# Signs of converted weights: a rectifier of slope -2^32 on ScalarE in place of a VectorE step

## The chip, the cores and the metric

The kernel runs on one core of a Trainium2 chip. The time is the device time of one execution in microseconds (us). The engines are TensorE (PE in the profile, with PEld for its weight loads), VectorE (DVE), ScalarE (ACT), GpSimd (POOL) and SyncE (SP, which issues the DMAs).

## The reference

Attention with 4 batches, 8 heads, 576 positions and 64 dimensions per head, then two layers with hidden width 2048 on the 2304 tokens of width 512. The first layer's activation is Mish, the second's h * clip(h + 3, 0, 6) / 6.

```python
scores = scale * q @ k.T                     # scale = 1 / 8
thresh = max(scores, -1) - tau               # tau = 0.02
scores = where(scores >= thresh, scores, -1e9)
attn = exp(scores - max) / (sum + 1e-9)
x = (attn @ v) -> [2304, 512]
h = x @ w_in;  g = h * tanh(softplus(h));            x = g @ w_out      # first layer
h = x @ w_in2; g = h * clip(h + 3, 0, 6) / 6;        out = g @ w_out2   # second layer
```

## The kernel before

The matrix products run on float16 parts: each operand is split into a high part and the rest, and the products of the parts are added in PSUM. In the second layer sums and differences of quarters are multiplied in place of the quarters, so that its weights need combined parts (`combined`).

The weights lie in memory as float64 words of 64 bits. Each of the four matrices (m = 0 and 1 for the first layer, 2 and 3 for the second) is converted on the chip in 8 groups, so there are 32 conversions, all by `one_conversion`. For one group the 64-bit words are loaded (`raw`, tile raw_lr), DVE finds the largest magnitude (L785), and a scale for the group follows: a diagonal of the per-partition values (L756 on ACT or L758 on DVE, tile dgb_zd), a product with ones on PE that spreads it over partitions (L761), a maximum on DVE (L764) and a few short steps (L796 to L810). Then, into a tile of 128 x 1024 words (cvt_c):

- `c1`, ACT, L921: the high 32-bit halves, read as float32, times the group's scale.
- `c2`, POOL (L929) or DVE (L931), one half of the tile each: shift left by 3, which moves the exponent of float64 to the place of that of float32, and clears the sign bit.
- `c3`, DVE, L937: the sign bit of the raw words is put in.
- `c4`, DVE, L942: the top bits of the low 32-bit halves are put in.
- For m below 2, ACT makes the float16 high part (L961) and POOL or DVE the rest. For m = 2 and 3, sums of quarters (`q`), high parts on ACT (L997) and rests follow.

The work around it changes in time. From about 30 to 140 us the softmax of attention and the conversions of m = 0 run together: PE makes scores (L1849, s_s), DVE the maximum (L1858) and the thresholded step (L1871, e_ex), ACT the exponential (L1868). Up to about 414 us the conversions of m = 1 follow, beside attention and the first product of the first layer, whose results ACT or DVE scales (L1290 and L1292, he_t) and SP stores. From then to about 640 us `first_layer` runs its second half: per unit of 512 columns ACT computes Mish (L1327, hp_e), ACT the float16 high part (L1330, gs_h), DVE the rest (L1336, gs_h), and PE 24 matmuls (L1356, y_y); a block of tokens has 8 units, and there are 72. The results are split again for the second layer (L1111, L1117, L1128). The conversions of m = 2 and 3 lie in this stage, 16 in all. Then the second layer runs (L1430, L1458, L1517, L1523, L1533).

Each engine's instructions stand in an order that a planner (`Plan`) sets when the kernel is built: every step is a `task` with a cost per engine, dependencies, buffers and a due time, shifted by a table of numbers (`NUDGE`). The planner gives each step to the engine that it thinks free first. Engines execute their rows in that order and wait by semaphores. Tiles come from rings of a few buffers: hp_e has 2 in the late stage, gs_h 2 of 4 units each.

ACT computes by tables that it holds in sets. The kernel asks for one set at its start (L699), in which the exponential lies. The program loads another by an instruction of its own, ACT_TABLE_LOAD, where the next activation isn't in the set that ACT holds.

Of the kernel before, what the change touches and what calls it, by code (L numbers as in the profile page):

```python
# [8 lines left out]
F32 = mybir.dt.float32  # L9
# [6 lines left out]
AF = mybir.ActivationFunctionType  # L16
ALU = mybir.AluOpType
# [81 lines left out]
JOIN_FROM = 340.468  # L99
STAY = 0.954  # L100
NBLK_EARLY = 2 * B - 2
NUDGE = {
# [407 lines left out]
class Plan:  # L510
# [19 lines left out]
    def add(  # L530
        self, engines, fn, deps=(), bufs=(), prio=None, off=0.0, dma=0.0, name="", order=()
    ):
        shift = NUDGE.get(name, 0.0)
        prio, off = (None, off + shift) if prio is None else (prio + shift, off)
# [149 lines left out]
def fused_kernel(ctx: ExitStack, tc, q, k, v, tau, w1i, w1o, w2i, w2o, out):  # L684
    nc = tc.nc
# [42 lines left out]
    def sub(e, dst, a, b):  # L728
        engine[e].tensor_tensor(dst, a, b, ALU.subtract)  # L729

    def pick(which, **cost):
        return {e: cost[e] for e in WHO[which]}
# [14 lines left out]
    def bits(t):  # L747
        return t.bitcast(U32)
# [24 lines left out]
    wt, r_w, converted, scaled_by, wsc = {}, {}, {}, {}, {}  # L773

    def high(raw):
        return bits(raw.tile).rearrange("p a (n t) -> p a n t", t=2)[:, :, :, 1]
# [96 lines left out]
    def tasker(at):  # L873
        def task(engines, fn, deps, bufs, tag, dma=0.0):
            return add(engines, fn, deps, bufs, at, 0.0 if at is not None else MOE_OFF, dma, tag)

        return task
# [7 lines left out]
    def convert(m, src, pool, prio, off, ring):  # L885
        if m not in wsc:
            scale_columns(m)
        if m < 2:
            r_w[m] = Ring(f"w{m}_", maker(pool, f"w{m}_", [P, 2, 2, DM], F16), NG)
            wt[m] = [Buf(r_w[m]) for _ in range(NG)]  # L890
            for w in wt[m]:
                w.left += 1
        elif m == 2:
            r_w[m] = Ring(f"w{m}_", maker(pool, f"w{m}_", [P, 7, 2 * P], F16), 2 * NG)
        if m > 1:
            wt[m] = [(Buf(r_w[m]), Buf(r_w[m])) for _ in range(NG)]

        factors = []
        for g in range(NG):
            at = prio + 2 * g * off  # L900
            task = tasker(at)
            raw = Buf(r_raw)
            a = loaded = load_words(task, raw, src[g], f"lr{m}_{g}")
            a = maximum(task, f"{m}_{g}", raw, wsc[m]["top"][:, g : g + 1], a)
            factors.append(group_scale(task, f"{m}_{g}", m, g, ring, a))
            one_conversion(m, g, raw, [loaded, factors[g]], task)
        if m == 0:
            step = NG // len(scaled_parts)
            scaled_parts[:] = [factors[i : i + step] for i in range(0, NG, step)]
        scaled_by[m] = summary(tasker(prio + 2 * NG * off), m, ring, factors)  # L910

    def one_conversion(m, g, raw, deps, task):
        nm = f"{m}_{g}_"
        t = Buf(r_cvt)
        dst = wt[m][g]

        def low():
            return bits(raw.tile).rearrange("p a (n t) -> p a n t", t=2)[:, :, :, 0]

        def c1(e):  # L920
            nc.scalar.activation(  # L921
                t.tile.bitcast(F32), high(raw).bitcast(F32), AF.Copy,
                scale=wsc[m]["sc"][:, g : g + 1],
            )

        def c2(e, j):
            if e == "pool":
                ti = t.tile[:, j].bitcast(I32)
                nc.gpsimd.tensor_tensor(ti, ti, eight.to_broadcast([P, DM]), ALU.mult)  # L929
                return  # L930
            nc.vector.tensor_scalar(  # L931
                t.tile[:, j], t.tile[:, j], 3, 0x7FFFFFF8, ALU.logical_shift_left,
                ALU.bitwise_and,
            )

        def c3(e):
            nc.vector.scalar_tensor_tensor(  # L937
                t.tile, high(raw), 0x80000000, t.tile, ALU.bitwise_and, ALU.bitwise_or
            )

        def c4(e):
            nc.vector.scalar_tensor_tensor(  # L942
                t.tile, low(), 29, t.tile, ALU.logical_shift_right, ALU.bitwise_or
            )

        a = task(EXPAND, c1, deps, [raw, t], "c" + nm)
        b = [
            task(
                pick(f"c{m}{j}", **SHIFT) if m > 1 else SHIFT, lambda e, j=j: c2(e, j), [a], [t],
                f"c{nm}{j}",  # L950
            )
            for j in range(2)
        ]
        a = task({"dve": 1.28}, c3, b, [raw, t], "c" + nm)
        a = task({"dve": 1.28}, c4, [a], [raw, t], "c" + nm)
        if m > 1:
            combined(m, g, t, a, task)
            return

        def hi(e):  # L960
            nc.scalar.activation(dst.tile[:, :, 0], t.tile.bitcast(F32), AF.Copy)  # L961

        def lo(e, j):
            sub(e, dst.tile[:, j, 1], t.tile[:, j].bitcast(F32), dst.tile[:, j, 0])

        a = task({"act": 1.05}, hi, [a], [t, dst], "h" + nm)
        for j in range(2):
            converted[m, 2 * g + j] = task(
                {"pool": 1.25, "dve": 0.68}, lambda e, j=j: lo(e, j), [a], [t, dst], f"u{nm}{j}"
            )  # L970
# [289 lines left out]
    def inner(blk, early, at=None, gap=0.0):  # L1260

        task = planner(at, gap, f"0_{blk}")
        if blk == 2 * B:
            x, src = Buf(r_x), Buf(r_sum)

            def tails_of():
                return src.tile

            def get(e):
                nc.sync.dma_start(out=tails_of(), in_=td)  # L1270

            a = task({"sp": 0.5}, get, tails, [src], "xt", 1.46)
            ready = [
                split(task, f"0_{blk}", src, tails_of, x, xinv[:, B:], r_h, [a])
            ]
            input_scales(B, ready[0], None if at is None else at)
        else:
            x, ready = x_of.pop(blk)
        hscale, scaled = hin[:, blk // 2], hin_done[blk // 2]
        for fp in range(NG):  # L1280
            h = Buf(r_h)
            last = gemm1(task, 0, fp, PIECE if early else 12, x, h, ready)
            if fp % 2 == 0:
                he = Buf(r_he)
                taken = []

            def take(e, h=h, he=he, fp=fp):
                dst, f = he.tile[:, fp % 2], hscale[:, fp : fp + 1]
                if e == "act":
                    nc.scalar.activation(dst, h.tile, AF.Copy, scale=f)  # L1290
                else:
                    nc.vector.tensor_scalar(dst, h.tile, f, None, ALU.mult)  # L1292

            taken.append(task(TAKE, take, [last, scaled[fp]], [h, he], f"t{fp}", 0.0, fp + VECTOR))
            if fp % 2:

                def put(e, he=he, fp=fp):
                    nc.sync.dma_start(out=hd[blk][:, fp // 2], in_=he.tile)

                h_stored[blk, fp // 2] = task(  # L1300
                    {"sp": 0.5}, put, taken, [he], f"s{fp}", HD_DMA, fp + VECTOR
                )
# [761 lines left out]
    t = 0  # L2064
# [3 lines left out]
    for b in range(B):  # L2068
        units = [(hp, cs) for cs in halves for hp in range(NPAIR)]
        tiles = {}  # L2070
        for i, (hp, cs) in enumerate(units):
# [4 lines left out]
            t = tiles[hp](t, cs)  # L2076
# [3 lines left out]
            blk = 2 * b + (i == len(units) - 1)  # L2080
            if (i == len(units) - 1 or i == NPAIR - 1) and blk < NBLK_EARLY:
                pending.append((blk, START + (t + MOE_LAG) * STEP, span * STEP * RATE / NG))
    for blk in range(NBLK_EARLY, NBLK):
        inner(blk, False)
# [60 lines left out]
    task = tasker(at)  # L2145
# [81 lines left out]
```

## Time and profile before

| | |
|---|---|
| median of 3 runs | 985.71 us (985.18 to 986.22) |
| the profiled execution | 984.73 us, span 982.9 us |
| PE busy | 922.2 us (94%) |
| DVE busy | 797.9 us (81%) |
| ACT busy | 650.8 us (66%) |
| POOL busy | 409.2 us (42%) |
| mean granted clock of TensorE | 0.974 |

The span is that of the instructions on the core; the execution's own time is 1.8 us longer. Busy time is a sum over an engine's instructions. An engine that is busy for all of a stretch sets its length; one that is idle there has a reason, which the waits name.

### The profile page before, as it was taken

Reading aid. Unit: us, or ns where it says so; the run is one execution under the profiler, and the core shown is the slowest. Engines: PE = TensorE matmul, PEld = TensorE weight load, DVE = VectorE, ACT = ScalarE, POOL = GpSimd, SP = SyncE. Lnnn points to the kernel's source line nnn. Section 1 sums busy time; section 2 is a strip of 40 time slices with the busy share of each in tenths; the row PEclk is TensorE's granted clock in tenths of the full one; section 3 lists DMA queues with packets and bytes.
Section 4 is the critical chain, followed back from the end, with each engine's and each line's share of the span. In section 5 each row is a group of like instructions: output and inputs, shape, how many; then the busy total and the mean of one; then the engine's idle time right before and its main releaser. Section 6 shows DMA issues by size and latency. Waiting matters only on the chain.

```text
span 982.9 us, 25896 instructions
## 1 busy us (share of the span) xinstructions
PE 922.2 (94%) x10776; PEld 797.2 (81%) x10776; DVE 797.9 (81%) x1516; ACT 650.8 (66%) x1051; POOL 409.2 (42%) x354
## 2 busy tenths in 40 slices
PE   3669779999999999999999999999999999999996
PEld 1447457777777778888888888899999999999986
DVE  6998898888878888569999889888758758758864
ACT  6678688888888877567866778655444444545541
POOL 2777776766655667315656777720000000000000
PEclk9769789999999999999999999999999999999999
DMA  9899999999999999864654757750110110110001
GB/s 313 179 233 234 228 226 218 251 253 217 238 217 270 216 220 238 234 239 173 239 211 176 282 188 287 246 219 9 60 47 16 60 41 22 60 32 31 23 15 31
DMA packets 201798, 164.48 MB, mean 167 GB/s; under 512 B 174160, under 2 KB 174928, under 8 KB 195280
## 3 DMA queue, kind: packets, MB, share of 16 engines
q1 hardware_dynamic: 201680, 162.82, 61.1%
q8 instruction: 85, 1.39, 0.6%
q14 instruction: 33, 0.27, 0.1%
HBM read 84.28 MB, written 36.04 MB: 122 GB/s over the span
## 4 chain that ended last, share of the span: by engine, by line
PE 76%; DVE 13%; POOL 3%; DMA 3%; issue 2%; ACT 1%; SPq 0%; DVEq 0%; POOLq 0%; ACTq 0%
PE h_g L1241 15%; PE y_y L1356 13%; PE s_s L1849 7%; PE aux_pv L1897 5%; PE hp_g1a L1430 5%; PE h_g0a L1430 5%; PE hp_g1d L1430 2%; PE h_g0d L1430 2%; DMA pt_tr<-p_ph 2%; DVE e_ex L1871 2%; DVE nm_pk L1858 1%; POOL p_ph L729 1%; DVE top L785 1%; PE h_g1b L1430 1%; DVE gs_h L1336 1%
## 5 line engine op out<-in xcount | busy, mean ns | idle before, releaser
L729 POOL TENSOR_TENSOR p_ph<-e_ex,p_ph 128x128 f16<-128x128 f32 (+3 forms) x160 | 192.5, 1225 | 106.4 <-issue 54.8
L1583 PEld LDWEIGHTS <-gs_h 128*128 128x128 f16 x1512 | 146.8, 98 | 18.0 <-issue 1.5
L1430 PEld LDWEIGHTS <-w__h 128*128 128x128 f16 x2016 | 156.0, 98 | 1.2 <-issue 0.6
L1871 DVE SCALAR_TENSOR_TENSOR e_ex<-s_s,thr_th,e_ex 128x576 f32<-128x576 f32 x144 | 111.9, 812 | 15.3 <-ACT thr_th L1863 11.8
L1858 DVE TENSOR_REDUCE nm_pk<-s_s 128x1 f32<-128x576 f32 x144 | 104.6, 751 | 18.0 <-PE s_s L1849 17.0
L1868 ACT ACTIVATE e_ex<-s_s,nm_pk 128x576 f32<-128x576 f32 x144 | 104.1, 730 | 18.5 <-DVE nm_pk L1858 13.9
L1849 PE MATMUL s_s<-kd_lk,qs_qp 64*128 64x288 f32 x440 | 80.8, 480 | 36.4 <-DVE e_ex L1871 25.6
L1876 ACT ACTIVATE p_ph<-e_ex 128x576 f16<-128x576 f32 x144 | 94.8, 678 | 13.5 <-DVE e_ex L1871 9.1
L1430 PEld LDWEIGHTS <-w__u 128*128 128x128 f16 x1008 | 98.6, 98 | 0.0
L1897 PEld LDWEIGHTS <-pt_tr 128*128 128x128 f16 x2016 | 81.3, 103 | 11.1 <-issue 5.8
L1849 PEld LDWEIGHTS s_s<-kd_lk,qs_qp 64*128 64x128 f32 x440 | 41.4, 204 | 59.0 <-issue 39.5
L1897 PE MATMUL aux_pv<-vh,pt_tr 128*128 128x65 f16 (+1 forms) x1296 | 86.1, 203 | 1.9 <-DMA pt_tr<-p_ph 1.9
L729 DVE TENSOR_TENSOR gs_h<-g_ab,gs_h 128x896 f16<-128x896 f32 x72 | 74.6, 1087 | 15.9 <-ACT gs_h L1533 15.9
L1533 ACT ACTIVATE gs_h<-g_ab 128x1792 f16<-128x1792 f32 x36 | 59.6, 1690 | 27.4 <-DVE g_ab L729 27.4
L1897 PE MATMUL aux_pv<-vl_vl,pt_tr 128*128 128x64 f16 x720 | 70.7, 203 | 0.0
L1517 ACT ACTIVATE g_ab<-g_ab,aux,hscales 128x512 f32<-128x512 f32 x72 | 54.1, 804 | 16.9 <-DVE g_ab L1458 16.9
L1327 ACT ACTIVATE hp_e<-hl_l 128x512 f32<-128x512 f32 x72 | 42.4, 594 | 23.5 <-DVE gs_h L1336 23.2
L1290 ACT ACTIVATE he_t<-h_g,hin 128x512 f32<-128x512 f32 x63 | 42.9, 683 | 19.0 <-PE h_g L1241 15.1
L1523 DVE SCALAR_TENSOR_TENSOR g_ab<-g_ab,f 128x512 f32<-128x512 f32 x72 | 51.2, 747 | 5.0 <-ACT g_ab L1517 5.0
L1336 DVE SCALAR_TENSOR_TENSOR gs_h<-hp_e,fscales,gs_h 128x512 f16<-128x512 f32 x72 | 53.0, 743 | 2.1 <-ACT gs_h L1330 2.1
L1330 ACT ACTIVATE gs_h<-hp_e,fscales 128x512 f16<-128x512 f32 x72 | 47.3, 678 | 7.6 <-PE y_y L1356 6.8
L1448 ACT ACTIVATE s_ka<-h_g0a 128x512 f32<-128x512 f32 x27 | 16.1, 595 | 48.1 <-PE h_g0a L1430 47.9
(672 smaller groups left out, 2559.2 us busy)
## 6 DMA issues: line engine op xcount, KB each, us to landing
hd<-he_t SPq DMA_DIRECT2D x36, 512.0 KB, 4.2
hl_l<-hd SPq DMA_DIRECT2D x18, 1024.0 KB, 5.7
raw_lr<-in_moe_w_in SPq DMA_DIRECT2D x16, 1024.0 KB, 6.0
raw_lr<-in_moe_w_out SPq DMA_DIRECT2D x16, 1024.0 KB, 7.5
yd<-yl_zhy SPq DMA_DIRECT2D x9, 896.0 KB, 3.8
qs_qp<-in_q SPq DMA_DIRECT2D x10, 576.0 KB, 5.8
v_lv<-in_v SPq DMA_DIRECT2D x16, 320.0 KB, 4.7
kd_lk<-in_k SPq DMA_DIRECT2D x15, 288.0 KB, 3.9
```

What stands on the lines that cost most here:

```text
L729: engine[e].tensor_tensor(dst, a, b, ALU.subtract)
L1241: mm(hv[:, j, :], wj[:, wl, c * P : (c + 1) * P], x.tile[:, c, xl, :], start=j == 0 and n == 0, stop=j == 1 and n == 11, skip_group_check= ...
L1336: nc.vector.scalar_tensor_tensor(s.tile[:, k, 1], g.tile.rearrange("p (a n) -> p a n", a=2), fs[:, fp : fp + 1], s.tile[:, k, 0], ALU.mult ...
L1356: mm(yv[:, h, :], wt[1][f // 2].tile[:, f % 2, wl, c * P : (c + 1) * P], gs[fp // COL].tile[:, fp % COL, gl, f % 2, :], start=fp == 0 and ...
L1430: mm(dst.tile[:, i * Q : (i + 1) * Q], wt[2][fp][wl].tile[:, right - 1, c * P : (c + 1) * P], x[xl].tile[:, c, left - 1], start=first and ...
L1583: mm(region(p), part[:, gl, left - 1], wt[3][fp][wl].tile[:, right - 1], start=fp == n == 0 and spot(p)[1] == 0, stop=fp == NG - 1 and n == 2,
L1849: mm(s[j].tile[:, half, :HALF], lh[r], rh[r], start=m == 0, stop=m == len(terms) - 1,)
L1858: nc.vector.tensor_reduce(neg.tile[:, j : j + 1], sv(j), AX.XY, ALU.max, negate=True)
L1868: nc.scalar.activation(ev(j), sv(j), AF.Exp, bias=neg.tile[:, j : j + 1])
L1871: nc.vector.scalar_tensor_tensor(ev(j), sv(j), thr.tile[:, j : j + 1], ev(j), ALU.is_ge, ALU.mult)
L1876: nc.scalar.activation(p16.tile[:, js, :S], e_.tile[:, js], AF.Copy)
L1897: mm(ov[:, dst, :d], pt.tile[:, j, ch, :], part.tile[:, src, vc, :], start=i == j == ch == 0 and part is vh, stop=j == w - 1 and ch == 8, ...
```

## The change

`c1` becomes a parametric rectifier (Prelu): with the group's scale applied, positive values stay, and negative ones are multiplied by -2^32. So the result is never negative, and a value that was negative has an exponent larger by 32. The shift by 3 of `c2` moves that bit of the exponent to bit 31, the sign, and the mask on DVE now keeps it. `c3` is left out: its task stays in the plan with the same cost, and issues nothing.

```diff
+NEGATIVE = -(2.0 ** 32)
...
+    def idle(e):
+        pass
+
...
         def c1(e):
             nc.scalar.activation(
-                t.tile.bitcast(F32), high(raw).bitcast(F32), AF.Copy,
-                scale=wsc[m]["sc"][:, g : g + 1],
+                t.tile.bitcast(F32), high(raw).bitcast(F32), AF.Prelu,
+                scale=wsc[m]["sc"][:, g : g + 1], alpha=NEGATIVE,
             )
...
             nc.vector.tensor_scalar(
-                t.tile[:, j], t.tile[:, j], 3, 0x7FFFFFF8, ALU.logical_shift_left,
+                t.tile[:, j], t.tile[:, j], 3, 0xFFFFFFF8, ALU.logical_shift_left,
                 ALU.bitwise_and,
             )
-
-        def c3(e):
-            nc.vector.scalar_tensor_tensor(
-                t.tile, high(raw), 0x80000000, t.tile, ALU.bitwise_and, ALU.bitwise_or
-            )
...
-        a = task({"dve": 1.28}, c3, b, [raw, t], "c" + nm)
+        a = task({"dve": 1.28}, idle, b, [raw, t], "c" + nm)
```

The orders of PE, POOL and SP are the same. Lines of the changed kernel are shifted by one or so.

DVE, at the first conversion of m = 0 (cvt_c_0, in attention), before:

```order
L764 TENSOR_REDUCE top_146<-aux_zp_1_1_414 128x1
L1967 TENSOR_SCALAR den_dt_0_2_430<-aux_pv_0_0_1_306 128x4
L937 SCALAR_TENSOR_TENSOR cvt_c_0__1_377<-raw_lr_0_0_199,cvt_c_0__1_377 128x1024
L1970 RECIPROCAL den_dt_0_2_430<-den_dt_0_2_430 128x4
L799 TENSOR_SCALAR top_146<-top_146 128x1
L800 TENSOR_SCALAR sc_147<-top_146 128x1
```

The same place of DVE after the change:

```order
L765 TENSOR_REDUCE top_146<-aux_zp_1_1_414 128x1
L1966 TENSOR_SCALAR den_dt_0_2_430<-aux_pv_0_0_1_306 128x4
L1969 RECIPROCAL den_dt_0_2_430<-den_dt_0_2_430 128x4
L800 TENSOR_SCALAR top_146<-top_146 128x1
L801 TENSOR_SCALAR sc_147<-top_146 128x1
```

The row of `c3` is gone and its neighbours have closed up. So it is at all 32 conversions: DVE has 1422 rows in place of 1454.

ACT, at the last conversion of m = 2 (cvt_c_7, beside the Mish units hp_e of the first layer), before:

```order
L1330 ACTIVATE gs_h_0_4_1_8104<-hp_e_0_4_1_8090,fscales 128x512
L997 ACTIVATE w__h_6_0_2_8112<-cvt_c_6__1_7988 128x768
L921 ACTIVATE cvt_c_7__1_8130<-raw_lr_7_0_7903,sc_6626 128x1024
L1327 ACTIVATE hp_e_0_4_1_8164<-hl_l_0_4_0_7832 128x512
L997 ACTIVATE w__h_6_0_2_8112<-sum_q_6_0_1_8109 128x1024
L1117 ACTIVATE yl_zhy_2_0_2_1_8182<-xf_zvy_2_0_2_1_8059 128x1792
```

The same place of ACT after the change:

```order
L1329 ACTIVATE gs_h_0_4_1_8081<-hp_e_0_4_1_8067,fscales 128x512
L996 ACTIVATE w__h_6_0_2_8089<-cvt_c_6__1_7966 128x768
L925 ACT_TABLE_LOAD
L925 ACTIVATE cvt_c_7__1_8107<-raw_lr_7_0_7881,sc_6610 128x1024
L1326 ACT_TABLE_LOAD
L1326 ACTIVATE hp_e_0_4_1_8141<-hl_l_0_4_0_7811 128x512
L996 ACTIVATE w__h_6_0_2_8089<-sum_q_6_0_1_8086 128x1024
L1116 ACTIVATE yl_zhy_2_0_2_1_8159<-xf_zvy_2_0_2_1_8036 128x1792
```

The activations stand in the same order. A table load stands before the rectifier and one before the next Mish, and so at each of the 16 conversions of m = 2 and 3, some with a few activations between the rectifier and the second load. At the 16 conversions of m = 0 and 1 ACT has no new row. ACT has 977 rows in place of 945.

## Rows read from the trace of the kernel before

**Rows 1.** The page: busy us of each engine, its share, its instructions.

```profile
PE 922.2 (94%) x10776; PEld 797.2 (81%) x10776; DVE 797.9 (81%) x1516; ACT 650.8 (66%) x1051; POOL 409.2 (42%) x354
```

**Rows 2.** Busy time by stretch: length, PE, PEld, DVE, ACT, POOL, PEclk, DMA share, GB/s.

```profile
30.00:140.00 110.00, 79.94 (x821) 57.86 (x817) 99.41 (x210) 81.86 (x144) 80.85 (x74) 0.78 0.94 221
140.00:432.00 292.00, 289.73 (x3466) 231.91 (x3466) 240.18 (x447) 232.08 (x431) 174.66 (x157) 1.00 1.02 235
432.00:610.00 178.00, 175.81 (x1617) 157.23 (x1616) 164.92 (x278) 135.46 (x201) 118.21 (x84) 1.00 0.60 215
```

**Rows 3.** Waits from 30 to 140 us: total us, times, longest.

```profile
PEld s_s L1849 <- issue: 23.9, 17, 4.5
PE s_s L1849 <- DVE e_ex L1871: 19.9, 10, 4.1
PEld s_s L1849 <- DVE e_ex L1871: 5.4, 3, 4.7
```

**Rows 4.** Waits from 432 to 610 us.

```profile
ACT hp_e L1327 <- DVE gs_h L1336: 21.3, 23, 3.7
...
PE h_g L1241 <- DVE he_t L1292: 2.1, 1, 2.1
```

**Rows 5.** Busy time of L937 (`c3`) alone, by stretch: length, DVE, PEclk, DMA share, GB/s.

```profile
30.00:140.00 110.00, 10.82 (x8) 0.78 0.94 221
140.00:432.00 292.00, 9.72 (x8) 1.00 1.02 235
432.00:640.00 208.00, 24.09 (x16) 1.00 0.61 222
sum 610.00, DVE 44.63; mean DVE 14.88
```

**Rows 6.** Timeline of DVE at two early sign steps: start us, us; idle before.

```profile
34.23 1.23 DVE L937 SCALAR_TENSOR_TENSOR cvt_c__1_377<-raw_lr,cvt_c__1_377 128x1024 uint32<-128x1024 uint32 x1 [0.37 <-POOL cvt_c__1_377 L929]
35.37 0.17 DVE L1970 RECIPROCAL den_dt<-den_dt 128x4 f32<-128x4 f32 x1
...
111.29 1.43 DVE L937 SCALAR_TENSOR_TENSOR cvt_c__1_1405<-raw_lr,cvt_c__1_1405 128x1024 uint32<-128x1024 uint32 x1 [1.67 <-POOL cvt_c__1_1405 L929]
```

**Rows 7.** Chain of waits from 440 to 535 us: start us, us, what.

```profile
470.18 3.07 DVE cvt_c__1_7392 L937
...
494.37 3.14 DVE cvt_c__1_7780 L937
...
530.01 1.47 PE h_g L1241 x12
```

**Rows 8.** The page's costliest groups: busy us, mean ns; idle before, releaser.

```profile
L1517 ACT ACTIVATE g_ab<-g_ab,aux,hscales 128x512 f32<-128x512 f32 x72 | 54.1, 804 | 16.9 <-DVE g_ab L1458 16.9
L1327 ACT ACTIVATE hp_e<-hl_l 128x512 f32<-128x512 f32 x72 | 42.4, 594 | 23.5 <-DVE gs_h L1336 23.2
L1290 ACT ACTIVATE he_t<-h_g,hin 128x512 f32<-128x512 f32 x63 | 42.9, 683 | 19.0 <-PE h_g L1241 15.1
```

**Rows 9.** Timeline of ACT at its one table load after the start.

```profile
413.10 0.69 ACT L1290 ACTIVATE he_t<-h_g,hin 128x512 f32<-128x512 f32 x1 [1.98 <-PE h_g L1241]
413.81 1.28 ACT L1327 ACT_TABLE_LOAD   x1
415.10 1.12 ACT L1327 ACTIVATE hp_e<-hl_l 128x512 f32<-128x512 f32 x2
416.16 1.25 ACT L1330 ACTIVATE gs_h<-hp_e,fscales 128x512 f16<-128x512 f32 x2
```

**Rows 10.** Timeline of DVE and of PE: one Mish unit finished, then used.

```profile
605.07 0.73 DVE L1336 SCALAR_TENSOR_TENSOR gs_h<-hp_e,fscales,gs_h 128x512 f16<-128x512 f32 x1
...
610.14 2.78 PE L1356 MATMUL y_y<-gs_h,w__h__1_5966 128*128 128x256 f16 x24
```

**Rows 11.** Timeline of ACT and of PE: one diagonal written, then used.

```profile
475.61 0.39 ACT L756 ACTIVATE dgb_zd<-ident,top 128x128 bf16<-128x128 f32 x1
...
476.07 0.22 PE L761 MATMUL h_zp<-dgb_zd,ones 128*128 128x128 bf16 x1
```

## The prediction, made blind

> **What bounds the kernel now.** I read first the busy time of each engine [rows 1]: TensorE (PE) is busy for 922.2 of 982.9 us, 94%, so an operation taken off another engine is worth something only where PE waits. I therefore cut the span at the places where the converted weights are used, and read busy time by stretch [rows 2]. From 140 to 432 us PE is busy for 289.73 of 292.00 us, from 432 to 610 us for 175.81 of 178.00 us. Only from 30 to 140 us is it open: 79.94 of 110.00 us, with a mean granted clock of 0.78. So 2.3 and 2.2 us are all that a shorter VectorE (DVE) could win in the last two stretches, and the first is where it could win more. There PE waits 19.9 + 5.4 us for DVE's softmax step, and 23.9 us for nothing that the profile shows [rows 3].
>
> For the loss I read the other side of the same rows: from 432 to 610 us ScalarE (ACT) is busy for 135.46 of 178.00 us, so it is idle for 42.5 us. Its largest wait, 21.3 us in 23 pieces, is for DVE to have used the Mish tile [rows 4]. The ring of these tiles is short, so ACT can't run ahead there.
>
> **What is removed.** The 32 sign steps on DVE (L937) cost 10.82, 9.72 and 24.09 us in the three stretches, 44.63 us in all [rows 5]. An undisturbed one takes 1.23 us and the next instruction starts 1.13 us after it: 34.23 to 35.37 us [rows 6].
>
> *Early, eight steps.* 8 x 1.13 = 9 us of DVE time. The waits for POOL in front of two of them, 0.37 and 1.67 us [rows 6], also move to L942, which stands later. PE waits there for DVE (25.3 us) about as long as for nothing shown (23.9 us) [rows 3], so I count half: -4 us. The bounds are 0 (something else is late next: ACT's exponential, or the transfers, whose share in that stretch is 0.94 [rows 2]) and -10 us (all of it, and one wait).
>
> *Middle, eight steps.* PE has 2.3 us open in 292, so 0, with bounds -2 and 0. What covers the old step is PE's own work.
>
> *Late, sixteen steps.* 24.09 us of DVE. The two slowest stand with 3.07 and 3.14 us in the chain of waits that leads to PE's h_g at 530.01 us [rows 7], where PE has its one longer stop, 2.1 us behind DVE's L1292 [rows 4]. That stop can go: -2 us at most, the open time of PE.
>
> **What is added.** The activation itself has the same shape and also a scale from a tile. I price it like the Copy that it replaces. From the nearest rows: at 128x512 a Copy with a scale from a tile takes 683 ns, a Mish without one 594 ns, and a rectifier that takes scale and bias from tiles 804 ns [rows 8]. Carried to 128x1024 by doubling the differences that is between -0.18 and +0.24 us each, for 16 late ones -2.8 to +3.9 us of ACT time; I take 0, since the Copy row is the nearest in its operands.
>
> The order shows what else comes: 32 loads of an activation table, two around each of the late 16 conversions, one before the rectifier and one before the next Mish, and none in the first 16, where ACT still holds the set of the start. Before, there was one load at this place: he_t starts at 413.10 us and lasts 0.69, the load starts at 413.81 and lasts 1.28, the Mish starts at 415.10 [rows 9]. So it costs 1.28 us, 0.03 us of gaps, and the 0.06 us or so by which ACT's neighbours otherwise overlap (1.12 us of Mish from 415.10, next at 416.16): 1.37 us. 32 x 1.37 = 44 us on ACT, 41 of it from 432 to 610 us (15 of the 16 conversions), against 42.5 us of idle time. ACT would be about full there.
>
> The Trainium skill, "ScalarE: Activation LUTs", section "What ACT_TABLE_LOAD costs", gives 1283 ns for the load, as the trace has it, and adds a drain of about 1380 ns to each switch of sets. This trace shows no such drain at its one switch. By the page the 32 loads would take an estimated 85 us of ACT; the rival of the doubled load below is the mechanism, worked out from rows.
>
> *What the 41 us do to PE.* Queued behind a late conversion on ACT are the Mish (L1327) and its rounding (L1330) for the units to come, the diagonals for the group scales (L756, which PE's L761 waits for) and he_t (L1290, PE's h_g). Two kinds of slack stand against it. A finished Mish unit waits for PE: the unit that DVE finishes at 605.07 + 0.73 = 605.80 us is first used at 610.14, 4.3 us later [rows 10]. Over the 72 units that slack is 2.6 to 15.5 us, typically 8, and 5 near the end. The diagonal has none: at 475.61 us ACT writes it, at 476.07 PE multiplies by it, 0.07 us after its end [rows 11].
>
> I went down ACT's rows from 432 us, adding 2.75 us at each conversion, taking off each idle piece that the lag can fill, and letting DVE come 1.13 us sooner per conversion where ACT waits for it. ACT's lag then comes and goes by 2 to 6 us and reaches 8 near 605 us, against slack of 5. PE is stopped at diagonals by 0.7 and 1.0 us before 490, wins 2.1 at 530, loses 2.4 at 560, 0.9 at 582 and 0.3 at 606: net +3 us. That is with all of ACT's idle time usable. But half of it is a wait for the short ring, and a late ACT makes that ring late as well. With half of 42.5 usable, 44 - 21 - 6 of slack (diagonals get less, units more) gives +17. I take +8, a third of the way from +3 to +17, since the return load usually stands before a Mish for which ACT had been idle, and so is hidden well. Bounds: -2 (loads all in idle time) and +44 (none of them).
>
> **Sum.** -4 + 0 + 0 + 8 = +4 us on the profiled execution of 984.73 us: 988.7. The median of the runs, 985.71, stands 0.98 us above that execution, so 989.7 us.
>
> **Rivals.**
>
> *The loads vanish in idle time (faster).* For it: 42.5 us of idle against 41, return loads that wait for nothing, and DVE in two chains [rows 3, 7]. Against it: the diagonals without slack [rows 11]. Early -6, late -2: 985.7 - 8 = 978 us. It decides when ACT's lag stays below 4 us at the end of the stage.
>
> *ACT becomes the bound of the late stage (much slower).* Half its idle time is unusable: late +17, early -4, 985.7 + 13 = 999 us. For it: the wait on DVE that makes half of the idle time [rows 4]. It decides when ACT's busy share with the loads is above 95% and its waits don't shrink to a few us.
>
> *Each load takes twice its row.* If a switch in the middle of work also costs the time to empty ACT, as long again as the load, 32 x 2.57 = 82 us stand against 42.5 us of idle and 6 of slack: late +34, early -4, 985.7 + 30 = 1016 us. The one switch in the trace speaks against it [rows 9].
>
> *The saved steps don't reach PE early.* PE's early waits shift to ACT or transfers, 0 instead of -4: 994 us. It is inside the range of the forecast.
>
> **Chances.** Forecast, with its own range of 984 to 995 us: 0.49. Loads hidden, 978: 0.28. ACT the bound, 999: 0.17. Doubled load, 1016: 0.06. A measurement of this kernel tells 0.2%, about 2 us, from no change. Of the forecast's 0.49, 0.04 lies below 983.7, 0.12 within 2 us of before and 0.33 above; of the faster rival's 0.28, 0.24 below and 0.04 within. So faster 0.28, same 0.16, slower 0.33 + 0.17 + 0.06 = 0.56. The range from 978 to 1006 us leaves out half of the faster rival and the doubled load, 0.2 together.
>
> **What would show it.** In the profile after: 33 loads at or near 1.28 us from 413 us on, and no gap of a microsecond behind them; the rectifier at 1.22 us; no L937 on DVE, and DVE down by 45 us. Early: less wait of PE for e_ex, the stretch shorter by some 4 us. Late: ACT above 90% busy up to 610 us, its wait for DVE's L1336 down from 21.3 us to under 10, PE newly waiting for ACT's diagonals and, near 600 us, for DVE's L1336; the stop at 530 us gone. I am wrong if the late stretch keeps its length with ACT that full (slack was more than I counted), if PE loses over 15 us there, or if the early stretch doesn't shorten.

## The result, and the profile after

The changed kernel takes 995.1 us (median of 4 runs, 992.34 to 996.9) against 985.44 us of the kernel before, measured beside it: a ratio of 1.0098, 95% interval 1.0070 to 1.0126, 9.7 us slower. Forecast were 989.7 us, with a range from 978 to 1006 us. The direction was right, and the loss more than twice as large as forecast.

The profiled execution took 996.9 us, 12.2 us more than that of before. Busy time first (the page, as in [rows 1]):

```profile
PE 928.5 (93%) x10776; PEld 800.1 (80%) x10776; DVE 754.2 (76%) x1484; ACT 693.2 (70%) x1083; POOL 395.8 (40%) x354
```

DVE has lost 43.7 us and 32 instructions, ACT has gained 42.4 us and 32 instructions. The sum over both engines is almost the same, and the kernel is slower. By stretch, to be read beside [rows 2]:

```profile
30.00:140.00 110.00, 83.55 (x827) 59.73 (x824) 92.17 (x208) 84.65 (x148) 79.84 (x76) 0.78 0.95 223
140.00:432.00 292.00, 288.25 (x3451) 230.61 (x3450) 227.83 (x433) 229.38 (x426) 167.90 (x155) 1.00 1.04 234
432.00:610.00 178.00, 168.36 (x1515) 149.01 (x1514) 133.67 (x252) 162.94 (x215) 107.62 (x81) 0.98 0.56 201
```

In the late stretch PE is busy for 168.36 us instead of 175.81, and has done about a hundred matmuls fewer (x1515 and x1617). There ACT is busy for 92% of the time, against 76% before.

The loads, from the lines of ACT (name, count, busy us, mean ns, idle before):

```profile
L1326 ACT ACT_TABLE_LOAD x17 | 21.8, 1283 | 0.3
L925 ACT ACT_TABLE_LOAD x16 | 20.5, 1283 | 0.3
```

They are 33 after the one at the start, each of 1283 ns. The timeline of ACT at the first two late conversions (start us, us):

```profile
432.29 1.28 ACT L925 ACT_TABLE_LOAD   x1
433.58 1.22 ACT L925 ACTIVATE cvt_c__1_6944<-raw_lr,sc 128x1024 f32<-128x1024 f32 x1
434.71 0.39 ACT L757 ACTIVATE dgb_zd<-ident,sm_zm 128x128 bf16<-128x128 f32 x1
435.12 1.28 ACT L1326 ACT_TABLE_LOAD   x1
436.41 0.60 ACT L1326 ACTIVATE hp_e<-hl_l 128x512 f32<-128x512 f32 x1
436.95 1.25 ACT L1329 ACTIVATE gs_h<-hp_e,fscales 128x512 f16<-128x512 f32 x2
438.21 1.28 ACT L925 ACT_TABLE_LOAD   x1
439.51 1.23 ACT L925 ACTIVATE cvt_c__1_7001<-raw_lr,sc 128x1024 f32<-128x1024 f32 x1
440.76 1.28 ACT L1326 ACT_TABLE_LOAD   x1
442.05 0.60 ACT L1326 ACTIVATE hp_e<-hl_l 128x512 f32<-128x512 f32 x1
```

Behind each load the next activation starts at once: 432.29 + 1.28 us, then 433.58. The rectifier takes 1.22 us, as the Copy did. Four loads stand within 10 us, and the Mish that started at 435.92 us before starts at 442.05. The kernel was 0.54 us late already at its first Mish load (414.35 us, against 413.81 in [rows 9]), so the four loads cost 5.6 us of ACT, 1.4 us each.

The timeline of PE shows what comes of it. These are its only stops between 415 and 650 us (in brackets the idle time and its releaser), with the rows behind two of them:

```profile
454.43 0.22 PE L762 MATMUL h_zp<-dgb_zd,ones 128*128 128x128 bf16 x1 [1.41 <-ACT dgb_zd L757]
455.80 1.47 PE L1355 MATMUL y_y<-gs_h,w__h__1_3173 128*128 128x256 f16 x12
460.40 0.26 PE L762 MATMUL h_zpy<-dgb_zdy,ones 128*128 128x128 bf16 x1 [3.13 <-ACT dgb_zdy L757]
460.46 2.76 PE L1240 MATMUL h_g<-x_zh,w__h__1_538 128*128 128x256 f16 x12
463.02 3.15 PE L1355 MATMUL y_y<-gs_h,w__h__1_3953 128*128 128x256 f16 x24
...
567.51 0.22 PE L762 MATMUL h_zpy<-dgb_zdy,ones 128*128 128x128 bf16 x1 [2.62 <-ACT dgb_zdy L757]
...
589.86 0.22 PE L762 MATMUL h_zpy<-dgb_zdy,ones 128*128 128x128 bf16 x1 [2.48 <-ACT dgb_zdy L757]
589.92 2.62 PE L1355 MATMUL y_y<-gs_h,w__h__1_2705 128*128 128x256 f16 x12
592.33 3.34 PE L1355 MATMUL y_y<-gs_h,w__h__1_3173 128*128 128x256 f16 x24
```

All four stops are in front of the product that spreads a diagonal, and together 9.64 us. Behind the second and the fourth twelve matmuls take 2.76 and 2.62 us in place of 1.47, and the next 24 take 3.15 and 3.34 in place of the 2.78 of [rows 10]: 3.37 us more. The windows behind the second stop say why (same columns as [rows 2]):

```profile
460.00:464.00 4.00, 3.60 (x19) 2.58 (x19) 3.80 (x13) 3.97 (x7) 3.13 (x4) 0.57 0.56 215
464.00:468.00 4.00, 4.00 (x39) 3.60 (x38) 3.69 (x8) 3.97 (x8) 2.46 (x2) 1.00 0.01 4
```

After PE's stop the mean granted clock was 0.57, so PE ran mostly at the lower of its two levels, 1.2 GHz, and from 464 us at 2.4 GHz again. Behind the fourth stop it was 0.51 from 590 to 592 us.

PE runs the same rows in the same order in both kernels, so the starts of one row can be compared. The last diagonal of the stage, before and after:

```profile
642.37 0.22 PE L761 MATMUL h_zpy<-dgb_zdy,ones 128*128 128x128 bf16 x1 [0.45 <-DVE dgb_zdy L758]
```

```profile
654.54 0.22 PE L762 MATMUL h_zpy<-dgb_zdy,ones 128*128 128x128 bf16 x1 [1.00 <-DVE dgb_zdy L759]
```

Here PE is 12.17 us late, and the second layer behind it adds nothing to the 12.2 us. Stops and clock make 13.0 us, the longer stop at this last diagonal 0.55 us, the later start of the stage 0.54 us, and the 2.1 us stop of [rows 4] is gone: 12.0 us together.

### The profile page after: what moved, and what is told of

It reads as the page before. It is cut to its first block, busy times and chain, and to the rows that moved or that the text cites. A ratio compares the mean times of both kernels' runs of the same rounds, so it can differ in the third digit from the quotient of the medians.

```text
span 995.1 us, 25870 instructions
## 1 busy us (share of the span) xinstructions
PE 928.5 (93%) x10776; PEld 800.1 (80%) x10776; DVE 754.2 (76%) x1484; ACT 693.2 (70%) x1083; POOL 395.8 (40%) x354
## 4 chain that ended last, share of the span: by engine, by line
PE 75%; DVE 8%; DMA 6%; ACT 6%; issue 2%; POOL 2%; SPq 1%; DVEq 0%; ACTq 0%; POOLq 0%
PE h_g L1240 16%; PE y_y L1355 12%; PE s_s L1848 7%; PE aux_pv L1896 5%; PE hp_g1a L1429 5%; PE h_g0a L1429 5%; DMA pt_tr<-p_ph 3%; PE hp_g1d L1429 2%; PE h_g0d L1429 2%; DMA raw_lr<-in_moe_w_in 2%; DVE e_ex L1870 1%; PE h_g1b L1429 1%; DVE nm_pk L1857 1%; PE hp_g0b L1429 1%; PE y_y__1_8_0_15054 L1582 1%
## 5 line engine op out<-in xcount | busy, mean ns | idle before, releaser
L730 POOL TENSOR_TENSOR p_ph<-e_ex,p_ph 128x128 f16<-128x128 f32 (+3 forms) x160 | 186.0, 1184 | 114.9 <-issue 54.8
L730 DVE TENSOR_TENSOR gs_h<-g_ab,gs_h 128x896 f16<-128x896 f32 x72 | 74.6, 1087 | 15.9 <-ACT gs_h L1532 15.9
```

## The experiments

Each is compared with the kernel before on the same chip; ratios below 1 are faster.

**Loads alone.** The kernel before, with the start's set loaded ahead of each late Copy.

```diff
         def c1(e):
+            if m > 1:
+                nc.scalar.preload_act_table_set("natural_log_exp_and_others")
             nc.scalar.activation(
```

> The kernel before with nothing but the 32 table loads added: the set of the start is loaded ahead of each Copy of the late 16 conversions, so the next Mish loads its own again. Copy and the sign step stay. Theory (the loads make ScalarE late, and TensorE stops at diagonals that ScalarE writes): 994 to 1002 us, at least as slow as the changed kernel, since VectorE keeps its sign steps; stops of TensorE behind the diagonals at L756 of 1 to 4 us each. Rival (the loads lie in ScalarE's idle time, and the loss comes from the rectifier or from VectorE's shifted work): 985 to 988 us.

Measured: 1003.34 us against 986.69, ratio 1.0168 (1.0143 to 1.0193), 16.6 us slower. ACT's rows are in the order of the changed kernel. PE stops at the same kind of row, eight times up to 650 us, and once more at the last diagonal of the stage, where the stop is the longest. The longest four:

```profile
456.56 0.22 PE L761 MATMUL h_zp<-dgb_zd,ones 128*128 128x128 bf16 x1 [2.00 <-ACT dgb_zd L756]
...
569.29 0.22 PE L761 MATMUL h_zpy<-dgb_zdy,ones 128*128 128x128 bf16 x1 [2.61 <-ACT dgb_zdy L756]
591.74 0.22 PE L761 MATMUL h_zpy<-dgb_zdy,ones 128*128 128x128 bf16 x1 [2.59 <-ACT dgb_zdy L756]
...
659.43 0.22 PE L761 MATMUL h_zpy<-dgb_zdy,ones 128*128 128x128 bf16 x1 [3.14 <-DVE dgb_zdy L758]
```

So the loads are the whole loss, and more than it: the left-out sign steps give some of it back.

**Sign steps alone.** The changed kernel with Copy in the rectifier's place. The signs of the weights are lost; nothing else is left out.

```diff
-                t.tile.bitcast(F32), high(raw).bitcast(F32), AF.Prelu,
-                scale=wsc[m]["sc"][:, g : g + 1], alpha=NEGATIVE,
+                t.tile.bitcast(F32), high(raw).bitcast(F32), AF.Copy,
+                scale=wsc[m]["sc"][:, g : g + 1],
```

> The changed kernel with Copy in place of the rectifier: no loads, no sign step (the weights lose their signs; the amount of work is that of the changed kernel without its loads). Theory (loss by loads alone; the sign steps are worth the stop of 2.1 us at 530 us and little early): 982 to 985 us. Rival 1 (the early lead of 4 us that the changed kernel has at 113 us is worth its size without the loads): 979 to 981 us. Rival 2 (the loss isn't of the loads): 990 us or more.

Measured: 978.79 us, ratio 0.9920 (0.9900 to 0.9940), 7.9 us faster, just past the fast edge of the first rival, and beyond the theory. PE has no stop from 415 to 650 us in its profile.

**The rectifier early only.** `if m < 2:` around the new `c1`, the new mask and the missing `c3`.

> The rectifier only in the first 16 conversions, which add no load; the late 16 as before, with Copy and the sign step. Theory (the early lead is lost again before 430 us, to waits for the transposing DMAs and to TensorE at half clock): 984.5 to 986 us, no change. Rival (the lead of 2 to 4 us at 113 to 140 us reaches the end): 981 to 983 us.

Measured: 982.91 us, ratio 0.9960 (0.9946 to 0.9975), 3.8 us faster. My theory was wrong here: the early lead does reach the end. In the profiled execution PE reaches the old stop at 525.91 us, 4.1 us before the 530.01 of [rows 7]:

```profile
525.91 1.47 PE L1250 MATMUL h_g<-x_zh,w__h__1_1758 128*128 128x256 f16 x12 [2.12 <-DVE he_t L1301]
```

I had drawn the theory from the one profiled execution of the changed kernel, which had no lead left at 414 us. How much of the lead is left there differs from execution to execution: the first Mish load starts between 408.93 and 414.35 us in the nine profiled executions that have the early change in the old plan, and between 413.81 and 415.89 in the three without it. The means are 411.5 and 415.1 us. So the gain of nearly 4 us is one of averages, and a single execution can hide it.

Taken together: -3.8 us early, -4.1 us for the late sign steps (978.79 to 982.91), +16.6 us for the loads. The sum is +8.7, against 9.7 measured, a difference within the intervals.

**Diagonals on DVE.** The changed kernel, with the late stage's diagonals issued on DVE.

```diff
-            if e == "act":
+            if e == "act" and not late_stage:
                 nc.scalar.activation(dg.tile, ident, AF.Copy, scale=src())
```

> The changed kernel, with all loads, but the diagonals of the late stage (L757, 18 of them on ScalarE) made by VectorE at the same place in the plan. Theory (TensorE's four stops at 454, 460, 567 and 590 us, 9.6 us, and the half clock behind two of them, 3.4 us, come from ScalarE reaching these diagonals late): most of it goes, 984 to 989 us. Rival (ScalarE is the bound of the whole stage, and the next late row of it, the Mish units, takes over): 992 us or more.

Measured: 997.12 us, ratio 1.0107 (1.0080 to 1.0134). No gain; the theory falls as far as it blames the engine that writes the diagonals. PE stops at three of the four rows, now behind DVE:

```profile
454.75 0.22 PE L764 MATMUL h_zp<-dgb_zd,ones 128*128 128x128 bf16 x1 [3.81 <-DVE dgb_zd L761]
...
566.41 0.22 PE L764 MATMUL h_zpy<-dgb_zdy,ones 128*128 128x128 bf16 x1 [3.04 <-DVE dgb_zdy L761]
588.12 0.22 PE L764 MATMUL h_zpy<-dgb_zdy,ones 128*128 128x128 bf16 x1 [1.84 <-DVE dgb_zdy L761]
```

The waits of this kernel from 425 to 650 us name what DVE is doing before: it waits for ACT's high parts of the Mish units, ahead of the diagonal in its own order, and ACT waits for DVE's rests.

```profile
DVE gs_h L1337 <- ACT gs_h L1331: 21.6, 13, 3.5
...
ACT hp_e L1328 <- DVE gs_h L1337: 15.7, 19, 2.1
```

**Thirty us taken off ACT.** The changed kernel with the rounding of the second layer's weights on DVE (`nc.vector.tensor_copy` in place of the activation at L996).

> The changed kernel, with all loads and without the sign steps, but the 32 high parts of the second layer's weights (L996, 16 of 0.84 and 16 of 1.05 us, 30 us) are rounded by VectorE at the same place in the plan. Theory (ScalarE's full queue as a whole is late, not one kind of row): about 30 of its 44 added us are taken off again, TensorE's stops go, 977 to 984 us. Rival (VectorE, which waits for ScalarE's rows in its own order, passes the delay on as it did with the diagonals): 990 us or more.

Measured: 1004.72 us, ratio 1.0190 (1.0167 to 1.0214), 9 us slower than the changed kernel. The theory that ACT's load alone decides falls too; since the work went to DVE, the run doesn't price a less busy ACT by itself. From 432 to 610 us ACT is as busy as before the change and DVE less busy than in [rows 2], yet PE is busy for 11 us less:

```profile
432.00:610.00 178.00, 164.88 (x1476) 145.09 (x1474) 153.19 (x269) 134.39 (x181) 107.40 (x77) 0.98 0.54 193
```

Its waits in that window:

```profile
ACT hp_e L1326 <- DVE gs_h L1335: 24.2, 21, 3.7
...
DVE gs_h L1335 <- ACT gs_h L1329: 12.3, 8, 3.5
...
PE h_zpy L762 <- ACT dgb_zdy L757: 8.5, 5, 2.8
```

The two engines hand the Mish units to each other through the two-buffer ring of hp_e, each in a fixed order. As these waits show, what makes one late makes the other late, though neither is busy all the time.

**Two pairs of loads.** The kernel before with loads at groups 0 and 1 of m = 2 alone (`if m == 2 and g < 2:`).

> The kernel before with table loads around the first two of the late conversions alone, 4 loads in place of 32. The 32 alone cost 16.6 us. Theory (a delay of ScalarE costs where it meets a row that TensorE is waiting for; after the first two pairs it is 6 us late at 442 us, and TensorE stopped at 454 and 460 us): these two pairs cost a third of the whole, 4 to 7 us, 989.5 to 992.5 us. Rival 1 (each pair costs the same): 2 us, 987.5 to 988.5 us. Rival 2 (a few loads vanish in idle time, only the sum of all fills ScalarE): 985 to 986.5 us.

Measured: 993.0 us against 987.41, ratio 1.0057 (1.0034 to 1.0080): 5.6 us for 4 of the 32 loads, with ACT far from full. The stops are those of the changed kernel, and later idle time of ACT (its wait for DVE from 415 to 650 us is 24.4 us, against 23.2 before) doesn't give them back:

```profile
456.17 0.22 PE L761 MATMUL h_zp<-dgb_zd,ones 128*128 128x128 bf16 x1 [2.02 <-ACT dgb_zd L756]
462.40 0.27 PE L761 MATMUL h_zpy<-dgb_zdy,ones 128*128 128x128 bf16 x1 [3.39 <-ACT dgb_zdy L756]
```

**All but these two.** The changed kernel with Copy and the sign step at these two conversions.

> The changed kernel with Copy and the sign step at the first two late conversions alone (groups 0 and 1 of m = 2), so 28 loads and not 32. Theory (these two pairs make the stops at 454 and 460 us and the half clock behind them, 6 us): 6 us under the changed kernel's ratio of 1.010, so 1.002 to 1.006. Rival (every pair costs the same): 2 us under it, 1.007 to 1.009.

Measured: 988.07 us, ratio 1.0014 (1.0000 to 1.0028), 0.8 points below the changed kernel's 1.0098, or 8 us. By the two intervals that is 5 to 11 us, so the 6 us of the theory lie inside. The stops at 454 and 460 us are gone, those of 2.62 and 2.50 us near 560 and 582 us remain, and one of 1.01 us shows at 487 us, which the changed kernel doesn't have.

**Seven pairs, away from the stops.** The rectifier in the first 16 conversions, in groups 2 to 7 of m = 2 and in group 0 of m = 3.

```diff
+        sloped = m < 2 or (m == 2 and g > 1) or (m == 3 and g == 0)
...
-            if m < 2:
+            if sloped:
```

> The rectifier in the first 16 conversions and in seven of the late ones, groups 2 to 7 of m = 2 and group 0 of m = 3; Copy and the sign step in the other nine. Fourteen loads stand in ScalarE's queue, none of them at the pairs ahead of TensorE's four stops (groups 0 and 1 of m = 2; groups 1 and 2, 3 and 4 of m = 3). Ratios to the kernel before, which is near 986 us. Theory (the loads cost only in the few places where the next diagonal is used at once, elsewhere the slack takes them up): the early gain of 0.4% and part of the late one, 0.992 to 0.996, 978 to 982 us. Rival (every pair costs about 1 us, 16.6 us by 16): seven pairs at 1 us, less 0.25 us for each sign step that goes, bring 5 us, ratio 1.000 to 1.003.

Measured: 980.48 us against 987.12, ratio 0.9936 (0.9916 to 0.9956), 6.6 us faster than the kernel before and the lowest median in this study of a version that does the whole computation. Its interval overlaps that of the early-only version (0.9946 to 0.9975), so a gain from the seven late pairs isn't shown; that they cost 5 us is excluded. The fourteen loads bring PE one stop, and the 2.1 us of [rows 4] are gone:

```profile
485.79 0.22 PE L762 MATMUL h_zp<-dgb_zd,ones 128*128 128x128 bf16 x1 [1.03 <-ACT dgb_zd L757]
```

ACT is busy there for 154.53 of 178.00 us, 87%, and PE for 176.97, more than in [rows 2].

**Ten pairs.** Groups 5, 6 and 7 of m = 3 as well.

> As the version with seven late rectifiers, with groups 5, 6 and 7 of m = 3 as well: ten late pairs, twenty loads. TensorE had no stop behind these three in the changed kernel. Theory (local stops): the same as with seven or up to 1 us faster, ratio 0.990 to 0.996. Rival (every pair costs about 1 us): 3 us slower than with seven, ratio 1.002 to 1.006.

Measured: 984.47 us, ratio 0.9970 (0.9953 to 0.9987), 3.4 points in a thousand worse than with seven. The expectation of no cost was wrong. These pairs bring stops at the end of the stage:

```profile
622.68 0.22 PE L762 MATMUL h_zpy<-dgb_zdy,ones 128*128 128x128 bf16 x1 [0.58 <-ACT dgb_zdy L757]
627.84 0.22 PE L762 MATMUL h_zps<-dgb_zds,ones 128*128 128x128 bf16 x1 [1.02 <-ACT dgb_zds L757]
642.95 0.22 PE L762 MATMUL h_zpy<-dgb_zdy,ones 128*128 128x128 bf16 x1 [1.73 <-DVE dgb_zdy L759]
```

The third is the last diagonal, with 0.44 us in the version with seven pairs. The expectation had overlooked that the changed kernel stops there for 1.00 us; the other two rows don't stop it, perhaps since it is later there by other delays, which no run shows.

**A new plan.** The changed kernel with true costs in the plan: 2.75 us more for the late `c1`, no task for `c3`.

> The changed kernel with the planner told of the two changes: 2.75 us more for each late rectifier on ScalarE, and no task for the sign. The order of all engines comes out anew. Theory (the loss is of rows that an order made without the loads puts behind them): work is put elsewhere on ScalarE and the loads cost less, 980 to 990 us. Rival (the due times were set for the old costs, and a new order loses more than it gains): 991 us or more.

Measured: 1029.46 us, ratio 1.0440 (1.0410 to 1.0470). The time is that of the rival: PE waits at seven places for ACT's Mish units (13.7 us) and at five for DVE's (5.4 us), which it did nowhere in the late stage of the kernel before. The due times were set with the old costs; that this is the reason wasn't tested.

**he_t on ACT.** The early-only version with the late L1292 steps on ACT.

> The version with the rectifier in the first 16 conversions alone (982.9 us), and the last five steps of he_t that VectorE does after 415 us (L1292 of the kernel before) given to ScalarE at the same place in the plan. Theory (the stop of 2.1 us behind VectorE's he_t at 530 us can be taken away by itself): 980 to 981.5 us. Rival (he_t waits on ScalarE for something else as late): 982 to 984 us.

Measured: 983.1 us, ratio 0.9961 (0.9942 to 0.9979): no gain over the early-only version, the rival. The stop stays, with another name:

```profile
526.15 2.29 PE L1252 MATMUL h_g<-x_zh,w__h__1_1758 128*128 128x256 f16 x12 [2.45 <-ACT he_t L1301]
```

**The late stage by itself.** All versions but the replanned one have PE's rows in the same order. The change of the span, less the change of the start of the first Mish load, is what a version costs or gains from there on, without the differing early lead. It comes from one profiled execution of each. The early-only version has the late stage of the kernel before, and indeed no change there.

| version | first Mish load, us | span, us | from there on, us |
|---|---|---|---|
| kernel before | 413.81 | 982.9 | 0 |
| changed kernel | 414.35 | 995.1 | +11.7 |
| loads alone | 415.89 | 1001.6 | +16.6 |
| sign steps alone | 413.85 | 980.1 | -2.8 |
| early only | 409.66 | 978.8 | 0.0 |
| diagonals on DVE | 412.26 | 995.7 | +14.4 |
| thirty us taken off ACT | 408.93 | 1001.8 | +23.8 |
| two pairs of loads | 415.48 | 991.6 | +7.0 |
| all but these two | 411.72 | 987.2 | +6.4 |
| seven pairs | 410.44 | 978.2 | -1.3 |
| ten pairs | 412.53 | 983.5 | +1.9 |
| he_t on ACT | 409.60 | 980.8 | +2.1 |

## Why the prediction was right in direction and too small

*Early, -4 us: right on average.* The early-only version measures -3.8 us. In the profiled execution of the changed kernel the lead was lost again before 414 us, as the fourth rival has it (994 us, near the 995.1 measured); the nine executions above speak against it as a rule.

*Late sign steps, -2 us at most: not refuted.* By the medians they are worth 4.1 us, by the two intervals about 1.5 to 6.5 us, and 2.8 us in the profiled execution. There the stop at 530 us went, as said, and the 0.45 us at the last diagonal (642.37 us) too, which lay beyond the window of the bound, 432 to 610 us.

*The added activation at nothing: right.* The rectifier takes 1.22 us, as the Copy did.

*A load at 1.37 us: right.* ACT's rows fall back by 1.4 us at each of the first four loads, and in the changed kernel no load is followed by a gap. The page that adds a drain (the Trainium skill, "ScalarE: Activation LUTs", "What ACT_TABLE_LOAD costs") isn't borne out in any of the 33.

*What the loads do to PE: the step that failed in size.* The forecast for the late stage was +8 us net. The runs show 9.7 + 3.8 = 13.5 by the medians, and the profiled execution 11.7. The +8 was a third of the way from +3 (all of ACT's idle time usable) to +17 (half of it), on the ground that the return load usually stands before a Mish for which ACT had been idle. The rows of the kernel before don't bear this out: before 13 of the 16 Mish rows in question ACT had no idle time, before the other three 0.15, 1.06 and 0.25 us. The first two of them:

```profile
433.12 0.58 ACT L1327 ACTIVATE hp_e<-hl_l 128x512 f32<-128x512 f32 x1
...
435.92 0.59 ACT L1327 ACTIVATE hp_e<-hl_l 128x512 f32<-128x512 f32 x1
```

From 432 to 610 us ACT's idle time fell from 42.5 to 15.1 us, so 27.5 us of it took up loads: not all, and more than half. With that in the prediction's own sum, 44 - 27.5 - 6 is +10.5, near the 11.7 found.

The tally put 0.7 and 1.0 us at two stops before 490 us. The profile has 1.41 and 3.13 us and 1.66 us of half clock there, and the runs price the two pairs ahead of them at 5.6 to 8 us. The tally followed ACT's lag to the diagonals, but not around the loop through DVE and the transfers. The transfer of a next group's words, before:

```profile
439.90 0.33 SPq L881 DMA_DIRECT2D raw_lr<-in_moe_w_in  x1
```

The same transfer in the changed kernel, and what comes of it:

```profile
444.07 1.22 DVE L941 SCALAR_TENSOR_TENSOR cvt_c__1_6944<-raw_lr,cvt_c__1_6944 128x1024 uint32<-128x1024 uint32 x1
445.32 0.33 SPq L882 DMA_DIRECT2D raw_lr<-in_moe_w_in  x1
...
451.54 1.22 DVE L786 TENSOR_REDUCE top<-raw_lr 128x1 f32<-128x1024 f32 x1 [1.80 <-DMA raw_lr<-in_moe_w_in]
...
453.98 0.40 ACT L757 ACTIVATE dgb_zd<-ident,top 128x128 bf16<-128x128 f32 x1 [0.15 <-DVE top L797]
...
454.65 2.20 DVE L730 TENSOR_TENSOR w__u<-cvt_c__1_6944,w__h 128x768 f16<-128x768 f32 x1
...
457.54 0.60 ACT L1326 ACTIVATE hp_e<-hl_l 128x512 f32<-128x512 f32 x1 [2.18 <-DVE gs_h L1335]
...
459.95 0.40 ACT L757 ACTIVATE dgb_zdy<-ident,sm_zmy 128x128 bf16<-128x128 f32 x1
```

The late rectifier makes DVE's last step on the group (`c4`, L941) late. The next transfer into the words' ring starts 0.03 us after that step ends, in both kernels, and so 5.4 us later than before. DVE waits 1.80 us for its words, and the maximum that started at 445.09 us before starts at 451.54. For it ACT waits 0.15 us with the diagonal behind the first stop; ACT's own late rows would have brought it nearly as late, since the row before it ends at 453.83 us. Before the second stop ACT waits 2.18 us for DVE to free a Mish tile, behind a step of DVE (L730) that takes 2.20 us in place of 0.95; why it is longer isn't shown. So ACT comes to the next diagonal at 459.95 us, although its value was there at 454.07. An idle piece of ACT that is a wait for DVE isn't free to fill: DVE, late itself, ends it later.

The half clock behind two stops, 3.4 us in the profiled execution, was in no term.

*The stops' places* came out near the tally's: 560 us (2.4 us forecast, 2.62 found at 567.51 on the later clock), 582 us (0.9 forecast, 2.48 found). The 0.3 us at 606 isn't there. I had also expected PE to wait for a Mish unit near 600 us; none of them stopped it. ACT's wait for DVE's L1336 was to fall from 21.3 us to under 10 and fell to 10.5 in the same window.

*The rivals.* That the loads vanish in idle time is wrong, shown by the loads alone. That each load takes twice its row is wrong. That ACT is the bound, at 999 us, is nearest in size but for the fourth, but its sign, a busy share above 95%, didn't show (92%), and four loads of the 32, with ACT far from full, already cost 5.6 us.

## What to carry to other kernels

Count a change's new instructions from the order of the engines, and price each where it stands: two of sixteen equal pairs made a third or more of the loss here, and seven others cost nothing that the medians show. Time that two engines wait for each other isn't free time: with a ring of two buffers between them a delay in one comes back through the other. Before giving work to another engine because it has idle time, look what stands behind it in that engine's order, and try the change only at the places with slack.

## What the runs showed that I had not expected

- A stop of PE costs more than its length: behind stops of 3.13 and 2.48 us the granted clock fell (mean 0.57 from 460 to 464 us) and the next 36 matmuls took 1.66 and 1.71 us longer; behind the stop of 2.62 us at 567 us they took 2.78 us for 24, as usual.
- Leaving out 32 DVE steps of 1.13 us brought 7.9 us (0.8%; interval 0.6 to 1.0%), with PE at 94% busy before.
- The same thirty us of work, moved from ACT at 92% busy to DVE at 75%, made the kernel 9 us slower.
